# A mask table with three rows a partition: written to DRAM row by row sixteen times, read back by one DMA

## The chip, the core and the metric

The kernel runs on one core of a Trainium2 chip. The metric is the device time of one execution in microseconds: 312.74 us, the median of 3 runs (312.53 to 312.8) of the kernel before the change.

## The reference

The program computes a block-sparse attention and, on its output, a residual MLP layer. Inputs: q, k, v of 4 batches x 8 heads x 768 tokens x 64, three sampled key blocks for each of 24 blocks of 32 queries, and the MLP's weights.

```python
scores = scale * np.matmul(q, k.transpose(0, 1, 3, 2))
mask = np.abs(blk_i - blk_j) <= window          # neighbours, first and last block, sampled blocks
scores = np.where(mask, scores, -1000000000.0)
attn = np.exp(scores - max); attn = attn / (attn.sum + 1e-09); attn @ v

a1 = alpha1 * x + beta1                         # x: 4 x 768 x 512, the heads side by side
tok = np.einsum('ts,bsd->btd', w_tok, a1)
u = x + lam * tok
a2 = alpha2 * u + beta2
ch = np.maximum(a2 @ w_ch1, 0.0) @ w_ch2        # 512 -> 2048 -> 512
return u + lam * ch
```

The mask depends on the query block and the key block alone, and is the same for all batches and heads.

## The kernel before

**Tiling.** Token 6p+o lies in partition p, slot o. The 32 heads are worked on in 16 pairs. A pair's scores, keys on the partitions, are cut into nine units of 1,024 columns, two PSUM banks each. For each unit TensorE makes scores (L729 or L850), ScalarE takes the exponential into an f16 tile eT (L744 or L802), and TensorE multiplies eT with the values (L769 or L883), whose extra column of ones gives the sum; VectorE divides (L701, L704).

**Two ways to mask.** For pairs 0 to 5 the mask is in the matmul: 24 extra rows of the query operand hold 0 or -400 for each key block, and 24 extra rows of the key operand choose the block (operand rows 64 to 87, which `MB` names). For pairs 6 to 15 the two heads of a pair run side by side in a unit, and after the exponential VectorE takes the minimum of eT and a mask table, maskT, whose entries are 0 or 65504 (L807).

**The mask table.** maskT has 128 x 9 x 512 entries, that is six rows of 768 a partition, one for each slot o. It is made in three steps. `mrow` (L551) turns the 24 mask rows of a query operand into 0 and 65504 in partitions 64 to 87 of the same tile. `mout` (L557) stores these 24 rows in DRAM. `min_` (L569) reads them back with 18 DMAs on SP's queue: each fills eight partitions, 16 apart, with one row up to six times over. The tokens of partitions c, c+16, c+32, ... have the same places in their blocks of 32, so that one strided DMA does for eight partitions; two of the sixteen groups cross a block's border and take two DMAs.

**Operands by transposes.** Pairs 0 to 5 get their operands through TensorE transposes (L294) and copies (L363, L361). From pair 6 on, VectorE casts the loaded q and k into a staging tile rel (L584), and SP issues two transposing DMAs, q and k, into the operand tiles (L670). The same kind of DMA (L1010) transposes the input of the MLP from batch 1 on.

**MLP.** Token mixing is L962 (its residual add L972, its weights transposed at L506 from a load at L442), the first channel matmul L1044 with relu at L1057 (ScalarE) or L1061 (VectorE), the second L1106, the last sum L1123 and the store L1130. w2b is scaled on VectorE (L536) after its load (L472).

**Order.** A planner inside the kernel's source simulates five engines with assumed durations, and writes each engine's instructions in the order of its simulation. It also gives out the eight PSUM banks (six in one tile, one in another, one for the values' sums) and, where its model says that TensorE would stand, adds zero matmuls (`fill`, L252). `bank_order` and `pin_order` then fix the waits between engines and the order on each. SP's queue holds, in this order: the first loads, two copies of mask rows into operand tiles, mout, the 18 reads of min_, the two transposes of pair 6, those of pair 7, and then transposes and stores mixed. Loads of q, k, v and weights are issued by GpSimd (L399, L442, L464, L472), and from pair 8 on each waits for a flag that VectorE sets (L417, L397).

Of the kernel before, what the change touches and what calls it, by code (L numbers as in the profile page):

```python
# [18 lines left out]
B = 4  # L19
# [13 lines left out]
NPAIR = H // 2  # L33
VW = D + 2
UN = 1024
NU = 9
NS = NPAIR * NU
NPE = 6
NET = 11
LEADS = (18, 18, 18, 18, 18, 18, 18, 18, 19, 18, 18, 18, 18, 18, 18, 18)  # L40
PATS = (800.0, 800.0, 800.0, 800.0, 1200.0, 800.0, 0.0, 800.0, 800.0, 400.0, 800.0, 800.0, 800.0, 800.0, 800.0, 800.0)
NUDGE = {}
LOADS = (
    "v 0", "q 1", "k 1", "v 1", "q 2", "k 2", "tok 0", "tok 1", "tok 2", "v 2", "lam", "a1",
    "b1", "q 3", "v 3", "k 3", "a2", "be2", "q 4", "k 4", "v 4", "w1 0", "w1 1", "w1 2",
    "w1 3", "q 5", "k 5", "v 5", "q 6", "k 6", "v 6",
)
PR = 1
EARLY = ('b0', 'b1')
OLD = True  # L50
MROW = (2, 3, 9)
W2AT = (0, 1, 2, 7.5)
NSPLIT = 0
UTN = 0
TOKP = 1
COVER = 800.0
NLD = 6
HOLD = 2
T0 = 6600.0
MASK_AT = 28  # L60
AHEAD = 13000.0
SCALE = 1.0 / 8.0
EXPB = -0.35667494
F16MAX = 65504.0

# [71 lines left out]
def kernel(  # L137
# [69 lines left out]
    maskT = pp.tile([P, NU, 512], F16, name="maskT", tag="maskT")  # L207
# [8 lines left out]
    ps6 = ps.tile([P, 6 * 512], FP, name="ps6", tag="ps6", bufs=1)  # L216
    ps7 = ps.tile([P, 512], FP, name="ps7", tag="ps7", bufs=1)
    ps6_name = [ps6[:].tensor.name]
    BANKS = tuple(f"b{i}" for i in range(6))
    ALL = BANKS + ("b6",)  # L220
    PAIRS = ("b0+b1", "b2+b3", "b4+b5")

    def bank(name, shape, dt=FP):
        t = ps7[:, :] if name == "b6" else ps6[:, ts(ALL.index(name), 512)]
        if dt != FP:
            t = t.bitcast(dt)
        t = t[:, 0 : int(np.prod(shape[1:]))]
        return t if len(shape) == 2 else t.rearrange("p (o c) -> p o c", o=shape[1])

    def two_banks(names):  # L230
        return ps6[:, ts(PAIRS.index(names), UN)]

# [17 lines left out]
    def keep_warm(n, w, name="b6"):  # L250
        for _ in range(n):
            nc.tensor.matmul(bank(name, [P, w]), warm[:, 0:P], warm[:, 0:w], start=True, stop=True)  # L252

    def fill(ns):
        free = [x for x in ("b6", "b0", "b1") if slots[x] > 0]
        while ns > 60.0 and free:
            w = min(512, int(ns * 2.4))
            keep_warm(1, w, free[0])
            ns -= w / 2.4 + 3.0

    keep_warm(7, 512)
    keep_warm(2, P)
# [17 lines left out]
    rel0 = wk.tile([P, 2, NT, 2 * D], BF, name="rel", tag="rel", bufs=3)  # L280

    def first_cast(a):
        for i, src in enumerate((q2f, k2f)):
            sl = src[:, a, :].rearrange("p (o d) -> p o d", o=NT)
            dst = rel0[:, a, :, i * D : (i + 1) * D]
            if a == 0 and i == 1:
                nc.scalar.copy(out=dst, in_=sl)
            else:
                nc.vector.tensor_copy(out=dst, in_=sl)

    def transposes(rel, a, name, slots=range(NT)):
        tps = bank(name, [P, NT, P], BF)
        for o in slots:
            nc.tensor.transpose(tps[:, o, :], rel[:, a, o, :], identb[:])  # L294
        return tps.rearrange("p o c -> p (o c)")
# [3 lines left out]
    flatA = transposes(rel0, 0, "b0", range(0, 3))  # L299
    flatB = transposes(rel0, 0, "b1", range(3, 6))  # L300
    bqs = []
    for w in range(2):
        t = ps.tile([P, 512], FP, name="ops", tag="ops", bufs=1) if w else bank("b2", [P, 512])
# [15 lines left out]
    keep_warm(7, P)  # L319
    for j in range(2, NQB):  # L320
# [4 lines left out]

    ACT_COPY = dict(ACT=790.0)
    dma_free = [8000.0]
    SEM = 70.0  # L330
    DRAIN = 166.0
    free_at = dict(NEVER=1e9, NONE=0.0, PE=T0, ACT=T0, DVE=T0, POOL=4800.0, SP=T0)
    slots = dict(
        **{b: 1 for b in ALL}, ops=1, eT=NET, head=NQB, vext=NV, ld=NLD, rel=3,
        x=NXB, uT=3, hts=2, a1p=2, ub=2, ot=2, w2b=1,
    )
    jobs = []
    now = [0.0]

    class Job:  # L340
        def __init__(self, eng, dur, prio, fn, deps=(), take=(), give=(), lat=None):
            self.eng = eng if isinstance(eng, tuple) else (eng,)
            self.dur, self.prio, self.fn = dur, prio, fn
            self.deps = list(deps)
            self.take, self.give = take, give
            self.lat = lat
            self.alt = {}
            self.xfer = None
            self.late = 0.0
            self.moves = False  # L350
            self.done = None
            self.gate = None
            self.marks = []
            self.n = len(jobs)
            if prio in NUDGE:
                self.prio = (prio[0] + NUDGE[prio],) + prio[1:]
            jobs.append(self)

    def copy(eng, out, in_):
        if eng == "ACT":  # L360
# [4 lines left out]
    def Copy(prio, fn, deps, take=(), give=(), only=False):  # L365
        j = Job(("DVE", "NEVER") if only else ("ACT", "DVE"), 550.0, prio, fn, deps, take, give)
        j.alt = ACT_COPY
        return j

    def pieces(u):  # L370
        f = u * 512
        while f < (u + 1) * 512:
            jt, c = divmod(f, S)
            w = min(S - c, (u + 1) * 512 - f)
            yield f - u * 512, jt, c, w
            f += w

    def mmt(n, cols):
        return n * (max(cols, 60) / 2.4 + 2.7)

    def dve(n, rate, base):
        return base + n / 0.96 / rate

    pairs = [(b, n) for b in range(B) for n in range(NPAIR)]
    tl = {}
# [3 lines left out]
    def Load(xfer, prio, fn, deps=(), take=()):  # L389
        j = Job("POOL", 720.0, prio, fn, deps, take)  # L390
        j.xfer = xfer
        return j

    def load(name, src_ap, shape, dt, tag, bufs, xfer, prio, deps=(), take=(), held=None):
        def fn():
            if held is not None:
                nc.gpsimd.tensor_copy(out=held_[0:1, held : held + 1], in_=flag[0:1, held : held + 1])  # L397
            t = wk.tile(shape, dt, name=name, tag=tag, bufs=bufs)
            nc.gpsimd.dma_start(t[:], src_ap)  # L399
            return t  # L400

        return Load(xfer, prio, fn, deps, take)

    ld = {}
    wload = {}
    w2tile = []
    wtk_tile = []

    after = []
    flag = pp.tile([P, 3 * len(pairs)], BF, name="flag", tag="flag")  # L410
    held_ = pp.tile([P, 3 * len(pairs)], BF, name="held", tag="held")

    def raise_flag(p, i):
        c = 3 * p + i

        def fn():
            nc.vector.memset(flag[0:1, c : c + 1], 0.0)  # L417

        j = Job("DVE", 70.0, (0, p), fn)
        after.append((j, (p - 2) * NU + HOLD + 3 * i))  # L420
        return [j]

    def load_pair(p, prio, which="qkv"):
        for i, (src, dt, nm) in enumerate(((q, BF, "q2"), (k, BF, "k2"), (v, F16, "v2"))):
            if p == 0 and nm != "v2" or nm[0] not in which:
                continue
            hold_ = p > NPE + 1
            ld[p, nm] = load(
                nm, pair_ap(src, *pairs[p]), [P, 2, NT * D], dt, "ld", NLD,
                1300.0 if p < 2 else 980.0, prio, raise_flag(p, i) if hold_ else [], take=("ld",),  # L430
                held=3 * p + i if hold_ else None,
            )
            ld[p, nm].late = 1500.0 if hold_ else 0.0

    def plain(eng, dur, prio, fn, deps=(), **kw):
        return Job(eng, dur, prio, fn, deps, **kw)

    def load_wtk(g, prio):
        def fn():
            if g == 0:  # L440
                wtk_tile.append(wk.tile([P, NT, S], BF, name="wtk", tag="w2b", bufs=1))
            nc.gpsimd.dma_start(  # L442
                wtk_tile[0][:, 2 * g : 2 * g + 2, :],
                moe_w_tok.rearrange("(p o) s -> p o s", o=NT)[:, 2 * g : 2 * g + 2, :],
            )

        wload["tok", g] = Load(2100.0, prio, fn, take=("w2b",) if g == 0 else ())

    def load_bc(t, src, prio):
        def fn():  # L450
            nc.gpsimd.dma_start(t[:], src.unsqueeze(0).to_broadcast([P, DM]))

        return Load(720.0, prio, fn)

    def load_be2(prio):
        def fn():
            with nc.allow_non_contiguous_dma(reason="512 elements"):
                nc.gpsimd.dma_start(be2T[:], moe_beta2.rearrange("(o p) -> p o", p=P))

        return Load(200.0, prio, fn)  # L460

# [33 lines left out]
    for p in range(7, len(pairs)):  # L495
        load_pair(p, len(LOADS) + p)

# [898 lines left out]
```

## Time and profile before

| what | value |
|---|---|
| median of 3 runs | 312.74 us |
| profiled execution, first to last instruction | 307.7 us |
| its own time, launch and end included | not given apart; the median is 5.0 us above the span |
| TensorE matmul busy | 298.9 us, 97% |
| VectorE busy | 207.5 us, 67% |
| ScalarE busy | 205.8 us, 67% |
| TensorE clock granted | 1.00 |
| DMAs on SP's and ScalarE's queues | 30,940 packets, 14.61 MB |
| DMAs of GpSimd's queue | 15,984 packets, 15.47 MB |

Times in the profile count from the first instruction of the program. PE is TensorE, PEld its weight loads, DVE VectorE, ACT ScalarE, POOL GpSimd, SP SyncE; a q behind an engine's name is its queue, which issues DMAs and waits. In a line of the order of time the numbers are start and duration in us, x the count, and in brackets the idle time before it with what ended it. In a line of waits the numbers are us in total, times, and the longest.

### The profile page before, as it was taken

How to read it: one execution, taken by the hardware profiler on the slowest of the kernel's cores; microseconds unless marked ns; L12 is line 12 of the kernel's file. 1: busy time of each engine (PE TensorE's matmuls, PEld its weight loads, DVE VectorE, ACT ScalarE, POOL GpSimd, SP SyncE). 2: the span in 40 equal slices, each digit the busy share in tenths (PEclk: the TensorE clock that was granted, in tenths of full speed). 3: DMA queues.
4: the chain of work that ended last, by engine and by line, in shares of the span. 5: the costliest groups of instructions: out<-in, count | busy, mean ns of one | idle time of the engine just before them, and what ended most of it. 6: DMA issues, size and time to landing. Idle time of an engine off the chain costs nothing.

```text
span 307.7 us, 7558 instructions
## 1 busy us (share of the span) xinstructions
PE 298.9 (97%) x3161; PEld 188.1 (61%) x3194; DVE 207.5 (67%) x435; ACT 205.8 (67%) x270; POOL 52.6 (17%) x91
## 2 busy tenths in 40 slices
PE   7999999998999999999999999999999999999995
PEld 3677788674655765565656665565756656555444
DVE  4688998987889986757988696888868730010111
ACT  5999987987787567756765857766858728428000
POOL 4747323001132121211221111120000000000000
PEclk9999999999999999999999999999999999999999
DMA  5999999996453768295275834465020120010121
GB/s 147 186 253 221 213 204 210 172 125 109 69 89 66 132 71 144 51 110 110 49 134 87 128 62 111 87 87 77 3 63 34 28 29 33 34 70 0 54 84 68
DMA packets 47174, 30.81 MB, mean 100 GB/s; under 512 B 27516, under 2 KB 43044, under 8 KB 47140
## 3 DMA queue, kind: packets, MB, share of 16 engines
q0 software_dynamic: 15984, 15.47, 32.5%
q1 hardware_dynamic: 30940, 14.61, 22.7%
q8 instruction: 25, 0.41, 0.5%
q10 hardware_dynamic: 216, 0.24, 0.2%
q14 instruction: 9, 0.07, 0.1%
HBM read 32.04 MB, written 6.33 MB: 125 GB/s over the span
## 4 chain that ended last, share of the span: by engine, by line
PE 89%; DMA 6%; POOL 2%; issue 1%; ACT 1%; DVE 0%
PE ps L1044 26%; PE ps L1106 21%; PE ps L962 10%; PE ops L883 8%; PE ps L850 7%; PE ps L729 5%; PE ops L1106 5%; PE ops L769 3%; DMA wtk<-in_moe_w_tok_dram 3%; DMA kx<-rel 3%; DMA q2f<-in_q_dram 1%; PE ps L506 1%; PE ps L294 1%; PE ps L252 1%; POOL v L399 0%
## 5 line engine op out<-in xcount | busy, mean ns | idle before, releaser
L802 ACT ACTIVATE eT<-ps 128x1024 f16<-128x1024 f32 x90 | 86.9, 1023 | 32.6 <-PE ps L850 28.6
L1044 PE MATMUL ps<-uT,w1b 128*128 128x384 bf16 (+1 forms) x512 | 93.1, 326 | 0.1
L1057 ACT ACTIVATE hts<-ps,b1t 128x384 bf16<-128x384 f32 x104 | 59.9, 581 | 37.9 <-PE ps L1044 32.2
L1106 PE MATMUL ps<-w2b,hts 128*128 128x512 bf16 (+1 forms) x293 | 72.4, 373 | 1.5 <-issue 0.2
L807 DVE TENSOR_TENSOR eT<-eT,maskT 128x1024 f16<-128x1024 f16 x90 | 60.4, 687 | 17.6 <-ACT eT L802 17.5
L1044 PEld LDWEIGHTS <-w1b 128*128 128x128 bf16 x512 | 46.3, 98 | 29.0 <-ACT eT L802 1.2
L1106 PEld LDWEIGHTS <-hts 128*128 128x128 bf16 x400 | 36.6, 98 | 36.1 <-issue 2.2
L744 ACT ACTIVATE eT<-ps 128x1024 f16<-128x1024 f32 (+1 forms) x55 | 52.2, 1019 | 4.8 <-PE ps L729 4.5
L883 PEld LDWEIGHTS <-eT 128*128 128x128 f16 x720 | 30.8, 97 | 15.1 <-issue 4.0
L962 PE MATMUL ps<-a1p,wtokT 128*128 128x128 bf16 x576 | 36.6, 219 | 0.0
L883 PE MATMUL ops<-vext,eT 128*128 128x65 f16 x720 | 36.0, 193 | 0.0
L962 PEld LDWEIGHTS <-wtokT 128*128 128x128 bf16 x576 | 33.3, 98 | 2.9 <-issue 0.5
L1123 DVE TENSOR_TENSOR ot<-x_sb,ps 128x512 f32<-128x512 f32 (+1 forms) x20 | 13.4, 672 | 28.3 <-PE ps L1106 28.3
L729 PE MATMUL ps<-qx,kx 88*128 88x512 bf16 (+1 forms) x144 | 31.4, 326 | 0.6 <-ACT kx L318 0.6
L397 POOL COPY held<-flag 1x1 bf16<-1x1 bf16 x24 | 9.4, 393 | 122.5 <-DVE flag L417 122.5
L850 PE MATMUL ps<-qx,kx 64*128 64x512 bf16 (+1 forms) x240 | 25.6, 326 | 1.2 <-DMA kx<-rel 1.2
L769 PEld LDWEIGHTS <-eT 128*128 128x128 f16 x432 | 18.3, 97 | 5.0 <-DVE x_sb L704 0.6
L769 PE MATMUL ops<-vext,eT 128*128 128x65 f16 x432 | 20.2, 193 | 0.1
L972 DVE TENSOR_TENSOR x_sb<-x_sb,ps 128x384 f32<-128x384 f32 x32 | 17.5, 550 | 3.9 <-PE ps L962 3.5
L704 DVE TENSOR_TENSOR x_sb<-ops,rcp 128x384 f32<-128x384 f32 x32 | 17.8, 558 | 1.1
L1123 DVE TENSOR_TENSOR ot<-x_sb,ops 128x512 f32<-128x512 f32 (+1 forms) x5 | 3.2, 634 | 22.5 <-PE ops L1106 22.5
L850 PEld LDWEIGHTS <-kx 64*128 64x128 bf16 x240 | 8.9, 94 | 14.7 <-issue 4.4
(68 smaller groups left out, 229.5 us busy)
## 6 DMA issues: line engine op xcount, KB each, us to landing
out_dram<-ot SPq DMA_DIRECT2D x23, 256.0 KB
v<-in_v_dram POOLq DMA_DIRECT2D x16, 192.0 KB, 5.3
q<-in_q_dram POOLq DMA_DIRECT2D x15, 192.0 KB, 3.8
k<-in_k_dram POOLq DMA_DIRECT2D x15, 192.0 KB, 4.8
w1b<-in_moe_w_ch_dram POOLq DMA_DIRECT2D x4, 512.0 KB, 9.9
w2b<-in_moe_w_ch_dram POOLq DMA_DIRECT2D x4, 512.0 KB, 14.7
wtk<-in_moe_w_tok_dram POOLq DMA_DIRECT2D x3, 384.0 KB, 9.6
maskT<-mask_rows SPq DMA_DIRECT2D x14, 72.0 KB
```

Of the source, the lines that this page charges most:

```text
L704: nc.vector.tensor_tensor(out=x_sb[:, s0 : s0 + NT, h * D : (h + 1) * D], in0=op[:, :, 0:D], in1=rcp[:].unsqueeze(2).broadcast_to([P, NT, D]),
L729: nc.tensor.matmul(sps[:, f - u * UN : f - u * UN + w], kx[h][0:KC, ts(jt, P)], qx[h][0:KC, c : c + w], start=True, stop=True,)
L744: nc.scalar.activation(eT[:, c], sps[:, c], AF.Exp, bias=EXPB, scale=SCALE)
L769: nc.tensor.matmul(ops[p, a][:, t * VW : t * VW + D + 1], eTs[p, u][:, ts(i - u * GU, P)], vx[:, a, jt, 0 : D + 1], start=(i % HT == 0), s ...
L802: nc.scalar.activation(eT[:], sps[:], AF.Exp, bias=EXPB, scale=SCALE)
L807: nc.vector.tensor_tensor(out=e, in0=e, in1=maskT[:, u, :].unsqueeze(1).broadcast_to([P, 2, 512]), op=ALU.min,)
L850: nc.tensor.matmul(sps[:, a * 512 + lo : a * 512 + lo + w], kx[sl][r, ts(jt, P)], qx[sl][r, c : c + w], start=True, stop=True,)
L883: nc.tensor.matmul(ops[p, a][:, t * VW : t * VW + D + 1], eTs[p, u][:, a * 512 + c * P : a * 512 + (c + 1) * P], vx[:, a, jt, 0 : D + 1], ...
L962: nc.tensor.matmul(tp[:, j, :], wtokT[:, s, ts(3 * g + j, P)], tl["a1p", p][:, s, :], start=(s == 0), stop=(s == NT - 1),)
L1044: nc.tensor.matmul(hp[:, 0:nc_], w1b[:, dk, ts(f, P)], uTs[b][:, dk, hf * HS : hf * HS + nc_], start=(dk == 0), stop=(dk == 3),)
L1057: nc.scalar.activation(hts[kk][:, f, :], hp[:, 0:HS], AF.Relu, bias=b1t[:, f : f + 1], scale=1.0)
L1106: nc.tensor.matmul(cps[kk, mi][:, 0:w], hts[kk][:, nk, ts(m, P)], w2tile[0][:, nk, lo : lo + w], start=(nk == 0), stop=(nk == 15),)
```

## The change

The mask table becomes 128 x 3 x 1024. Tokens 6p+2g and 6p+2g+1 lie in the same block, since 32 is even, so slots 2g and 2g+1 of a partition have the same mask row: three rows a partition are enough. A unit's 512 columns can begin at column 0, 512 or 256 of a row of 768 and run over its end, so each row is 1,024 long, and its last 256 columns repeat the first.

It is made in three steps again. `M` writes the 24 rows in two VectorE instructions, 768 and 256 columns. `N` is one DMA that stores each row sixteen times, one copy for each pair of tokens, as 384 rows of 1,024 in DRAM. `O` is one DMA that reads 128 x 3,072: rows 3p, 3p+1 and 3p+2 into partition p, which lie together in DRAM.

The planner is gone. What it wrote is now a table in the source, ORDER, of words such as `e54` (the exponential of unit 54), `q54:0` (its scores, in the first two banks) or `M0`, in the order in which instructions are written. Zero matmuls are words too (`z512:6`); eleven of their places have other widths or another number of them. All eight PSUM banks are in one tile, and bank_order handles them all.

```diff
-    maskT = pp.tile([P, NU, 512], F16, name="maskT", tag="maskT")
+    maskT = pp.tile([P, 3, UN], F16, name="maskT", tag="maskT")
...
-    ps6 = ps.tile([P, 6 * 512], FP, name="ps6", tag="ps6", bufs=1)
-    ps7 = ps.tile([P, 512], FP, name="ps7", tag="ps7", bufs=1)
+    psum = ps.tile([P, 8 * 512], FP, name="psum", tag="psum", bufs=1)
...
-    rows = maskT[:].rearrange("p u c -> p (u c)")[:, 0:S]
-    mask_dr = nc.dram_tensor("mask_rows", [NBLK, S], F16, kind="Internal").ap()
-    def mrow():
-        nc.vector.tensor_scalar(
-            out=rows[MB, :], in0=qx[3][MB, :], scalar1=-1.0, scalar2=F16MAX,
-            op0=ALU.is_ge, op1=ALU.mult,
-        )
-    def mout():
-        nc.sync.dma_start(mask_dr, rows[MB, :])
-    def min_():
-        dst = maskT[:].rearrange("p u c -> p (u c)").rearrange("p (o w) -> p o w", o=NT)
-        src = mask_dr.rearrange("(m f) w -> m f w", f=3)
-        for c in range(16):
-            o = 0
-            while o < NT:
-                f, r = divmod(NT * c + o, BLK)
-                e = min(NT, o + BLK - r)
-                nc.sync.dma_start(
-                    dst[c:P:16, o:e, :], src[:, f, :].unsqueeze(1).broadcast_to([8, e - o, S])
-                )
-                o = e
+    mask_dr = nc.dram_tensor("mask_rows", [S // 2, UN], F16, kind="Internal").ap()
+    rows = maskT[:, 0, :]
+    @on("M")
+    def _(_i):
+        for c, w in ((0, S), (S, UN - S)):
+            nc.vector.tensor_scalar(
+                out=rows[MB, c : c + w], in0=qx[3][MB, 0:w], scalar1=-1.0, scalar2=F16MAX,
+                op0=ALU.is_ge, op1=ALU.mult,
+            )
+    @on("N")
+    def _(_i):
+        nc.sync.dma_start(
+            mask_dr.rearrange("(m i) w -> m i w", m=NBLK),
+            rows[MB, :].unsqueeze(1).broadcast_to([NBLK, BLK // 2, UN]),
+        )
+    @on("O")
+    def _(_i):
+        nc.sync.dma_start(maskT[:], mask_dr.rearrange("(p g) w -> p g w", p=P))
...
-            def mn(p=p, u=u):
-                e = eTs[p, u][:].rearrange("p (a c) -> p a c", a=2)
-                nc.vector.tensor_tensor(
-                    out=e, in0=e, in1=maskT[:, u, :].unsqueeze(1).broadcast_to([P, 2, 512]), op=ALU.min,
-                )
+    @on("m")
+    def _(n):
+        e = eTs[n][:].rearrange("p (a c) -> p a c", a=2)
+        g, c = divmod(n % NU * 512, 2 * S)
+        mask = maskT[:, g, c % S : c % S + 512].unsqueeze(1).broadcast_to([P, 2, 512])
+        nc.vector.tensor_tensor(out=e, in0=e, in1=mask, op=ALU.min)
...
+    def zero(w, i):
+        nc.tensor.matmul(bank(i, [P, w]), warm[:, 0:P], warm[:, 0:w], start=True, stop=True)
+    @on("z")
+    def _(w, bank_):
+        zero(w, bank_)
+    for word in ORDER.split():
+        kind = word[: next(j for j, c in enumerate(word) if c.isdigit())]
+        n, _, arg = word[len(kind) :].partition(":")
+        args = (int(arg) if arg.isdigit() else arg,) if arg else ()
+        step[kind](int(n), *args)
```

## The prediction

> **What bounds the kernel now.** I read the page first, then TensorE's waits, then a table of stretches, then the order of time around the one hole that these show.
>
> ```profile
> span 307.7 us, 7558 instructions
> PE 298.9 (97%) x3161; PEld 188.1 (61%) x3194; DVE 207.5 (67%) x435; ACT 205.8 (67%) x270; POOL 52.6 (17%) x91
> ```
>
> TensorE is busy for 298.9 of 307.7 us, so at most 8.8 us can be won without taking work from it. Its waits (us in total, times, longest) say where they lie:
>
> ```profile
> PE ps L850 <- DMA kx<-rel: 1.2, 1, 1.2
> PE ps L252 <- DVE warm L248: 1.2, 1, 1.2
> PE ps L729 <- ACT kx L318: 0.6, 1, 0.6
> ```
>
> Two are in the first 7 us. The third is the first score group of pair 6 (L850), which waits for a transposing DMA. The table of stretches (us, then busy time of each engine) puts it in place:
>
> ```profile
> 31.60:70.10 38.50, 38.38 (x564) 30.27 (x566) 35.33 (x80) 34.27 (x41) 7.43 (x10) 1.00 1.16 182
> 70.10:71.30 1.20, 0.00 (x1) 0.01 (x2) 0.79 (x2) 0.06 (x1) 0.00 (x0) 1.00 1.29 274
> 71.30:304.20 232.90, 231.25 (x2238) 138.20 (x2266) 148.46 (x300) 144.04 (x198) 25.96 (x48) 1.00 0.40 73
> ```
>
> From 31.6 to 70.1 and from 71.3 to 304.2 TensorE is full at clock 1.00; in between it does nothing for 1.2 us. What holds it is on SP, whose queue and engines around it read, in order of time:
>
> ```profile
> 40.46 0.35 DVE L551 TENSOR_SCALAR maskT<-qx 24x768 f16<-24x768 bf16 x1
> 40.84 0.31 SPq L557 DMA_DIRECT2D mask_rows<-maskT  x1
> 45.17 16.39 SPq L569 DMA_DIRECT2D maskT<-mask_rows  x18
> 55.59 0.35 DVE L584 COPY rel<-k 128x768 bf16<-128x768 bf16 x1
> 62.01 1.32 SPq L670 DMA_TRANSPOSE qx<-rel  x1
> 63.46 2.54 SPq L670 DMA_TRANSPOSE kx<-rel  x1
> 69.07 1.02 PE L1106 MATMUL ps<-w2b,hts 128*128 128x512 bf16 x3
> 71.30 0.61 PE L850 MATMUL ps<-qx,kx 64*128 64x512 bf16 x6 [1.20 <-DMA kx<-rel]
> 73.25 0.69 DVE L807 TENSOR_TENSOR eT<-eT,maskT 128x1024 f16<-128x1024 f16 x1
> ```
>
> Pair 6's staging tile is complete at 55.94 (55.59 + 0.35), but SP is still issuing the 18 mask reads until 61.56, one each 0.91 us. So both transposes start 6 us after their data is there, and the table that they queue behind is first used at 73.25.
>
> **The change, part by part.** The built programs have the same order on all five engines except for the mask steps and eleven of the zero matmuls; the PSUM banks are the same too.
>
> *SP.* Eighteen issues (16.39 us) become one. The store that fills the DRAM table stays one issue (0.31; the transposes, with twice its packets, show 1.23, and I allow that). Queued behind on SP is only pair 6's transpose, due at 55.94. It starts there unless the new read, which waits for the new store, holds SP longer. Store: 384 packets of 2 KB instead of 24 of 1.5 KB. The trace's packet records give 0.087 us for a 2 KB packet of an output store (16 DMA engines, 128 packets, 1.2 us together), and show completion writes from 12 engines for the old store, from 8 for each mask read. Twelve engines with 32 packets: 2.8 us alone. Beside the weight loads of this stretch the mask packets took 0.15 instead of 0.078, so 5.6 us at double. The old store was issued at 40.84 and its first packet came at 44.4; 0.2 us later for the new DVE part, that gives an end at 47.4 to 50.2 and an issue of the read at 48 to 51. Read: 128 packets of 6 KB, eight per engine; the nearest rows are 0.25 us (token weights, 3 KB written from 6 KB) and 0.32 (w1, 4 KB from 8 KB), so 2.0 to 2.6 alone, 5.2 at double; with the 3.9 us that the first mask read took to its first packet, it ends at 54 to 60. The table is needed at 72: 12 us spare. SP is free by 51, 5 us before the transpose is due.
>
> The Trainium skill, "SBUF — State Buffer", section Door 1, speaks against this store: DMA rate depends on how many of 16 ports the partitions reach, and by its table partitions 64 to 87 reach six. At its 27.2 GB/s a port, an estimate from the page is 4.8 us for 786 KB, which lies inside 2.8 to 5.6 and changes nothing in the sum.
>
> *The two transposes.* They are issued at about 56.0 and 57.3 instead of 62.01 and 63.46. Alone, two such transposes (1536 packets of 256 B) took 1.9 us (104.2 to 106.1 in the packet records). Beside loads they crawl: from 78.5 to 80.5 one transpose went out with about one packet for each load packet. At 57 loads are still queued (w2 and pair 7, landing from 59.6 to 70.1). The mask reads of before sat on 8 engines, 99 packets of 0.078 each, 7.7 us; the new table costs 12 engines 2.8 + 2.0 = 4.8 and the other four 2.0, so the slowest engines get rid of their loads sooner. Bounds for the landing: 60 if the loads did not matter; 70.7 if the transposes came through only once the last load is off, as in before (loads off at 69.5; pair 6's last 650 packets then took until 70.4 and the first matmul came at 71.30, 0.9 later; with most packets already through, some 0.3 + 0.9 after 69.5). I take 67, nearer the upper end, because one packet for each load packet passes 96 per engine before the loads end.
>
> The Trainium skill, "DMA: Bandwidth & Descriptors", section Queues, rings and completion order, states that each DMA engine takes turns between queue rows packet by packet. That agrees with the interleaving above; taken strictly it would make the early transposes slow pair 7's load by one short packet each.
>
> *What TensorE gains.* The last L1106 matmul before the hole starts at 69.72 and takes 0.215; the next matmul after a change to L850 usually comes 0.095 later than its length asks. So pair 6 can begin at 70.03, against 71.30: **1.27 us**. Its PSUM banks are free (exponentials of the units before end at 69.2, the residual add on bank 1 at 68.34). What is late next: ScalarE's exponential of the unit before ends at 70.16, before the new scores are there; DVE is idle from 70.89 to 72.54; both wait for TensorE here and move with it. From 71.3 on nothing but TensorE's own work (231.25 of 232.90) sets the pace, so the shift lasts to the end, where the tail of 3.5 us after the last matmul is unchanged.
>
> *DVE.* One more tensor_scalar, 24x256: between 0.16 (the smallest DVE copies here) and 0.35 (24x768); 0.2. Behind it stands a residual add that waited 0.15 for TensorE, then the shift of pair 2's operand, used at 44.19 with 1.8 us to spare: 0. The min with the mask keeps its form, 90 x 0.687: 0.
>
> *Zero matmuls.* They shrink by 1,826 columns net; at 0.215 per 512 that is 0.77 us of TensorE. All but two lie before 31.4, where ScalarE runs without a hole (eight exponentials in 7.61 us from 25.08), and TensorE then waits 0.25 for it at 31.14: they become waiting. The two at 53.9 to 55.3 stand before transposes which start at 55.66, when ScalarE's copy of the last ones (54.78 + 0.80) frees the bank: 0. If those covers failed, the gain would be up to 0.13 for the latter, 0.64 for the former.
>
> *Waits.* The first score matmul now waits for ScalarE's step that ends at 6.10 instead of 6.59, up to 0.5 earlier; but TensorE stands at 17.6 for the token weights (landed 17.58), which don't move: 0. ScalarE's relus lose waits for DVE's; TensorE, which is full there, gains nothing.
>
> Sum: 307.7 - 1.27 = 306.4 of span. The runs' median is 312.74, 5.0 above the profiled span, and no time of that execution alone is given; I take the 5.0 as fixed: **311.5 us**.
>
> **The rivals.** A: *the transposes land late anyway.* If they come through only with the last load, at 70.7 at the latest, the gain is 0.6 or less: 312.1 to 312.7. For it: 63.3 to 69.5 shows them nearly stopped. Against: most of that stood behind mask packets until 66.6. B: *the store is the new wait* (slower). It reads each of 24 rows 16 times over; if these packets took turns instead of spreading over 12 engines, 384 x 0.087 = 33 us would put its end at 78, the read and the transposes behind it on SP, and the hole at some 15 us: 328. It decides from an end of the store at about 61, where SP is as late as now. Against: a packet of one partition took 0.078 as store or load. C: *pair 7's load.* It landed at 61.97 for a DVE cast at 62.56; the burst of mask and transposes comes ahead of it now. DVE has 0.72 idle behind that cast and TensorE about 0.5 more before it needs pair 3's operand (66.59). From a landing at 63.8 each us costs one. On the slowest engines the new table's 4.8 us and 96 transpose packets of 0.031 (3.0) now come before it, against some 72 mask packets of 0.078 (5.6) then: 2.2 us later at most, 64.2; I take half, 63.1. At 66 the gain is gone and 0.9 lost: 313.7. D: *more*, if the earlier start or the zeros count: 310.9.
>
> **How the numbers follow.** Full gain 0.67, A 0.16 (a quarter of it still beyond 0.2%), B 0.05, C 0.09 (half of it near no change), D 0.03. A measurement here can tell about 0.2%, 0.63 us. Faster: 0.67 + 0.04 + 0.03 = 0.74; within: 0.12 + 0.04 = 0.16; slower 0.10. The range goes from D, 310.9, over A into C, 312.9; the likeliest case alone spans 311.1 to 311.9.
>
> **What would show it.** Right: the page's PE wait on kx gone, SP's transposes for pair 6 at 56 to 57, TensorE's stretch from 31 to 303 without a hole, the span at 306.4. Wrong: an SP wait at the mask read past 56 (B), a DVE wait for q near 62.6 and TensorE idle near 66 (C), or a shorter wait on kx at 70 (A).

## The result, and the profile after

The kernel after takes 308.04 us (median of 4 executions, 307.76 to 309.19), the kernel before beside it 312.63 (311.66 to 312.8): a ratio of 0.9886 with a 95% interval of 0.9849 to 0.9924. Three later measurements of the unchanged pair gave 0.9887 [0.9856, 0.9919], 0.9889 [0.9859, 0.9919] and 0.9912 [0.9879, 0.9946]. The forecast was 311.5 with a range of 310.9 to 312.9. Its direction was right; its gain, 1.27 us, was less than a third of what came.

The first page of the kernel after:

```profile
span 306.0 us, 7521 instructions
PE 299.4 (98%) x3161; PEld 188.1 (61%) x3192; DVE 207.7 (68%) x436; ACT 205.7 (67%) x270; POOL 52.3 (17%) x91
```

TensorE's waits (us in total, times, longest) no longer hold one on kx:

```profile
PE psum L298 <- DVE warm L295: 1.2, 1, 1.2
PE psum L460 <- DMA wtk<-in_moe_w_tok_dram: 0.3, 1, 0.3
PE psum L792 <- issue: 0.2, 1, 0.2
```

The table of stretches (us, busy time of PE, PEld, DVE, ACT and POOL, then granted clock, DMA share, GB/s), cut where it was cut before:

```profile
31.60:70.00 38.40, 38.35 (x566) 30.21 (x566) 35.39 (x81) 33.95 (x41) 7.41 (x11) 1.00 1.22 208
70.00:71.30 1.30, 1.30 (x25) 0.83 (x25) 0.92 (x3) 1.00 (x2) 0.00 (x0) 1.00 0.00 0
71.30:302.60 231.30, 229.66 (x2215) 137.50 (x2242) 148.53 (x300) 143.33 (x198) 25.95 (x48) 1.00 0.41 72
```

The row in the middle is the old hole: TensorE was busy for none of it and is busy for all of it now. The order of time shows why, SP first, then TensorE:

```profile
52.63 0.35 SPq L506 DMA_DIRECT2D maskT<-mask_rows  x1
53.82 1.36 SPq L554 DMA_TRANSPOSE qx<-rel  x1
56.01 3.10 SPq L554 DMA_TRANSPOSE kx<-rel  x1
...
69.06 1.02 PE L792 MATMUL psum<-w2b,hts 128*128 128x512 bf16 x3
70.02 0.61 PE L595 MATMUL psum<-qx,kx 64*128 64x512 bf16 x6
```

Pair 6's transposes are issued 7 to 8 us earlier than at 62.01 and 63.46, and its scores begin at 70.02 instead of 71.30. So this profiled execution did what the forecast said (a span of 306.4), and its span is 1.7 us shorter than the one before (306.0 against 307.7). Yet the medians differ by 4.6 us. The experiments ask where the rest is.

In what follows every execution comes with its span, and its time is 1.72 to 1.84 us above it, in all 125 executions of the kernel before that were measured beside the experiments and all 20 of the kernel after. The 5.0 us that the forecast took for time outside the span are not there. The profiled execution of before (307.7, so some 309.5 us) lies at the low end of a kernel whose executions spread from 309.2 to 313.6 (clock is an execution's mean granted TensorE clock). Two executions of before, 314.5 and 315.1 us at a clock of 0.988, count as slow and are left out here and below:

```
kernel before, 123 executions: 309.2 to 310.9 us   27, clock 0.998 or more
                               310.9 to 311.2       2, clock 0.998 or more
                               311.2 to 312.9      49, clock 0.998 or more
                               310.0 to 313.6      45, clock 0.995 or less (median 312.5)
kernel after, 20 executions:   307.4 to 308.3      10, clock 0.998 or more
                               308.7 to 309.2      10, clock 0.998 or more
```

Over all of these the medians are 311.64 and 308.54, 3.1 us apart; that the first measurement gave 4.6 was in part a draw of long executions of before.

### The profile page after: what moved, and what is told of

Same layout as the page of the kernel before. It is cut to its first block, busy times and chain, and to the rows that moved or that the text cites. A ratio compares the mean times of both kernels' runs of the same rounds, so it can differ in the third digit from the quotient of the medians.

```text
span 306.0 us, 7521 instructions
## 1 busy us (share of the span) xinstructions
PE 299.4 (98%) x3161; PEld 188.1 (61%) x3192; DVE 207.7 (68%) x436; ACT 205.7 (67%) x270; POOL 52.3 (17%) x91
## 4 chain that ended last, share of the span: by engine, by line
PE 92%; DMA 4%; POOL 2%; issue 1%; ACT 1%; DVE 0%
PE psum L758 27%; PE psum L792 27%; PE psum L619 12%; PE psum L704 11%; PE psum L595 7%; PE psum L585 6%; DMA wtk<-in_moe_w_tok_dram 3%; DMA q2f<-in_q_dram 1%; PE psum L335 1%; PE psum L460 1%; POOL v L402 0%; PE psum L298 0%; POOL q L402 0%; POOL k L402 0%; PE psum L740 0%
## 5 line engine op out<-in xcount | busy, mean ns | idle before, releaser
L605 ACT ACTIVATE eT<-psum 128x1024 f16<-128x1024 f32 (+1 forms) x145 | 139.0, 1021 | 36.5 <-PE psum L595 27.6
L758 PE MATMUL psum<-uT,w1b 128*128 128x384 bf16 (+1 forms) x512 | 93.1, 326 | 0.1
L792 PE MATMUL psum<-w2b,hts 128*128 128x512 bf16 (+1 forms) x371 | 86.7, 370 | 1.6 <-issue 0.2
L772 ACT ACTIVATE hts<-psum,b1t 128x384 bf16<-128x384 f32 x104 | 60.4, 583 | 37.4 <-PE psum L758 33.4
L619 PE MATMUL psum<-vext,eT 128*128 128x65 f16 x1152 | 56.2, 193 | 0.0
L704 PE MATMUL psum<-a1p,wtokT 128*128 128x128 bf16 x576 | 36.6, 219 | 0.0
L585 PE MATMUL psum<-qx,kx 88*128 88x512 bf16 (+1 forms) x144 | 31.4, 326 | 0.1
L595 PE MATMUL psum<-qx,kx 64*128 64x512 bf16 (+1 forms) x240 | 25.6, 326 | 0.0
L653 DVE TENSOR_TENSOR x_sb<-psum,rcp 128x384 f32<-128x384 f32 x32 | 17.8, 558 | 1.1
L720 DVE TENSOR_TENSOR ub<-x_sb,a_bc 128x384 bf16<-128x384 f32 x32 | 17.7, 552 | 0.1
L595 PEld LDWEIGHTS <-kx 64*128 64x128 bf16 x240 | 8.9, 94 | 13.4 <-issue 4.5
```

The lines of the kernel that those rows point to most:

```text
L585: nc.tensor.matmul(t[:, f : f + w], kx[h][0:KC, ts(jt, P)], qx[h][0:KC, c : c + w], start=True, stop=True,)
L595: nc.tensor.matmul(t[:, a * 512 + f : a * 512 + f + w], kx[h][r, ts(jt, P)], qx[h][r, c : c + w], start=True, stop=True,)
L605: nc.scalar.activation(eTs[n][:, c], t[:, c], AF.Exp, bias=EXPB, scale=SCALE)
L619: nc.tensor.matmul(ops[p, a][:, t * VW : t * VW + D + 1], eTs[n][:, c : c + P], vext[p % NV][:, a, jt, 0 : D + 1], start=(jt == t == 0), s ...
L653: nc.vector.tensor_tensor(out=x_sb[:, s0 : s0 + NT, h * D : (h + 1) * D], in0=t[:, :, 0:D], in1=rcp[:].unsqueeze(2).broadcast_to([P, NT, D ...
L704: nc.tensor.matmul(t[:, j, :], wtokT[:, s, ts(3 * g + j, P)], a1p[p][:, s, :], start=(s == 0), stop=(s == NT - 1),)
```

## The experiments

In this part the table is ORDER, the planner's is the program that writes its order itself, and the hole is the stretch in which TensorE stands ahead of pair 6.

**Which part of the change does it?** Four kernels on one chip: before, after, and the two mixed ones. The old mask in the kernel with the ORDER table:

```diff
-    maskT = pp.tile([P, 3, UN], F16, name="maskT", tag="maskT")
+    maskT = pp.tile([P, NU, 512], F16, name="maskT", tag="maskT")
...
-        nc.sync.dma_start(maskT[:], mask_dr.rearrange("(p g) w -> p g w", p=P))
+        for c in range(16):
...
+                nc.sync.dma_start(
+                    dst[c:P:16, o:e, :], src[:, f, :].unsqueeze(1).broadcast_to([8, e - o, S])
+                )
```

> The table source with the old mask steps: one store of 24 rows and 18 reads; zero matmuls, banks and waits as changed. Theory 'mask alone': 312 to 312.8, as before, with TensorE's wait for pair 6's transposes back. Theory 'table': the gain beyond 1.3 us comes from the other zero matmuls and waits, so about 309.3. Theory 'outside': the time lies some 5 us above the span again if the number of DMAs issued decides that.

The new mask steps in the kernel with the planner (the same lines the other way):

> The planner's source with nothing but the mask steps changed (its order, zero matmuls and waits as before). Theory 'mask alone': 308 us, as the changed kernel. Theory 'table': 311.3 (1.3 us below before).

Before and after, unchanged:

> The kernel before, unchanged. The change took 4.6 us off the median where 1.3 us of the profiled span were forecast, and the changed kernel's executions all lie 1.8 us above their span. Theory 'body': the kernel before also spends 1.8 us outside its span, its usual executions have spans of 310 to 311 us, and the profiled one (307.7) was a lucky one; a new profile shows a longer wait than 1.2 us of TensorE for pair 6's transposes, up to 4.5. Theory 'outside': each execution's time lies 5.0 us above its span, spans stay at 307.7.

> The changed kernel, unchanged, on the same chip as the others: 308 us, span 306.2, time 1.8 us above its span, no wait for pair 6's transposes; one execution in four may be 1 us longer, as the first four were.

Measured, against the kernel before: unchanged 0.999 [0.9958, 1.0022]; old mask in the table 311.47 us, 0.9995 [0.9959, 1.0032]; new mask in the planner 308.17, 0.9928 [0.9888, 0.9968]; after 308.4, 0.9887 [0.9856, 0.9919]. The old mask keeps its wait in the table's program too:

```profile
PE psum L601 <- DMA kx<-rel: 1.2, 1, 1.2
```

The new profile of before, an execution of 309.74 us, has a wait on kx of 0.9 us, not the longer one that 'body' expected. In all four kernels time and span differ by 1.72 to 1.85 us, so what is won is won inside the span. In the medians the table alone brings nothing that can be told, the new mask most. But the new mask in the planner's program has two groups, six executions at 307.7 to 308.2 and four at 310.9 to 311.4; the kernel after has only the first and some near 309. That the source is worth nothing can't be said yet.

**What sets the executions of before apart?** Two more profiles of the unchanged kernel:

> The kernel before, unchanged, for another profiled execution. Executions of it took from 309.5 to 313.4 us, and about one in three reports a mean TensorE clock of 0.992 to 0.995 where the kernel after reports 0.999 to 1.000. Three theories for an execution above 311.3 us. CLOCK: the hole at pair 6 makes the clock fall to half for 3.4 us, so the profile shows a clock below 1.00 in a stretch after 70 us and about 1.7 us lost there. HOLE: the wait on kx is itself longer than in the first profile, 2.5 us or more instead of 1.2. START: the loss lies in the first 14 us, where TensorE reaches full rate later, and exponential 16 starts 2 us later than at 21.7. If this execution is a short one (309.5 to 310.5), all three say the same: a wait of 0.9 to 1.3 and no loss elsewhere.

> The same kernel and the same three readings as for b2_before_look: CLOCK a stretch after 70 us below full clock, HOLE a wait on kx of 2.5 us or more, START a late exponential 16.

The first caught one at a mean clock of 0.993 (311.76 us). Its wait on kx:

```profile
PE ps L850 <- DMA kx<-rel: 2.0, 1, 2.0
```

and its stretches (cut at the hole and where the clock changes):

```profile
66.00:69.90 3.90, 3.90 (x55) 2.72 (x53) 3.77 (x10) 3.29 (x4) 0.00 (x0) 1.00 1.33 115
69.90:73.35 3.45, 1.44 (x25) 0.91 (x25) 1.00 (x3) 1.08 (x3) 0.00 (x0) 1.00 1.07 108
73.35:76.77 3.42, 3.42 (x20) 1.54 (x18) 1.85 (x5) 2.58 (x4) 1.23 (x2) 0.50 0.21 26
```

The second row holds the hole; in the third TensorE is busy throughout, at a granted clock of 0.50. CLOCK holds for this execution, and HOLE in part: the hole is 0.8 us longer than in the first profile, and the fall behind it costs 1.57 us more (against the first profile its exponential 56 starts 0.69 later, exponential 60 then 2.26 later, and so to the end). Exponentials are counted here from 0, in the order in which ScalarE ran them, and serve as marks of how late an execution is. Below, an execution whose clock drops to half behind a hole has fallen.

The second profile, 311.5 us at a clock of 1.000, has no wait on kx:

```profile
PE ps L252 <- DVE warm L248: 1.2, 1, 1.2
PE ps L729 <- ACT kx L318: 0.2, 1, 0.2
```

Here exponential 16 starts at 24.95 instead of 21.67 (START). TensorE runs at half rate for longer; the same two matmuls in the first profile, and in this one:

```profile
8.79 0.60 PE L252 MATMUL ps<-warm 128*128 128x512 bf16 x2
```

```profile
11.29 1.06 PE L252 MATMUL ps<-warm 128*128 128x512 bf16 x2
```

This is called a late start below. TensorE comes to pair 6 3.28 us late, when the transposes have landed, and so gets 1.27 us back. So the long executions of before are, by these two profiles, of two kinds, and such a late start hides the hole.

**SP's issues, or the reads' load on the DMA engines?** The old 18 reads, with pair 6's transposes after the eleventh:

```diff
-r43 q46:2 S1 tq6 tk6 r44 e45
+r43 q46:2 S1 tq6 tk6 O1 r44 e45
...
+        for c, o, e, f in (reads[:11], reads[11:])[i]:
+            nc.sync.dma_start(
```

> The old table of 24 rows and its 18 reads, same bytes and packets as before, but pair 6's two transposes stand after the 11th read on SP instead of after the 18th. Theory ISSUE (SP's 16.4 us of issues held the transposes back): they are issued at 56 to 58, the wait on kx is gone or under 0.3 us, and the median is that of the kernel after, 308.0 to 308.6 us, with a clock of 0.999 to 1.000 in every execution. Rival LOAD (it is the old reads' packets on the DMA engines that keep the transposes from coming through, wherever they are issued): kx still lands after 69.5, the wait is 0.6 us or more, and the median is 310.5 to 311.6 as in the kernel before.

SP in order of time:

```profile
46.80 9.23 SPq L514 DMA_DIRECT2D maskT<-mask_rows  x11
56.55 1.54 SPq L562 DMA_TRANSPOSE qx<-rel  x1
58.20 3.23 SPq L562 DMA_TRANSPOSE kx<-rel  x1
61.48 7.24 SPq L514 DMA_DIRECT2D maskT<-mask_rows  x7
```

No wait on kx is left: their 1536 packets are out by 68.3, against the 69.1 that an early start would need (its scores can begin at 70.03, and the first matmul of before came 0.9 us behind the last packet). ISSUE holds in this, with all the old bytes still there, and no execution of 12 falls below a clock of 0.998. The time is 309.6 us, 0.994 [0.9909, 0.997], a microsecond more than expected; 0.44 of it is the end of the program, which is looked at last. The profiled execution had a late start (exponential 16 at 23.03). What else holds the others up was not looked at.

**What does a hole cost?** The kernel after, with the cast of pair 6's keys and their transpose put later:

```diff
-e42 r41 z384:6 H11:1 ck6 f0:0 cv6 ...
+e42 r41 z384:6 H11:1 f0:0 cv6 ...
-r43 q46:2 S1 tq6 tk6 r44 e45 ...
+r43 q46:2 S1 tq6 r44 e45 ...
-q53:1 x8 ... e53 S3 q54:0 q55:2 ...
+q53:1 x8 ... e53 S3 ck6 tk6 q54:0 q55:2 ...
```

> The kernel after with the cast of pair 6's keys, and their transpose, moved behind a later multiply on VectorE, so that the transpose is issued near 70 us and lands near 72.5: a hole of about 2.5 to 3.2 us comes back at pair 6, twice that of the kernel before, without its 18 reads. Theory CLOCK: the clock falls to half behind the hole in most executions, reported as 0.992 to 0.995, and the time is 308.2 + 2.9 + 1.7 = 312.8 us. Rival (the hole costs its own length and no more): 308.2 + 2.9 = 311.1 us at a clock of 0.999 to 1.000. If half of the executions fall, the times come in two groups 1.7 us or more apart.

```profile
71.00:73.82 2.82, 0.32 (x4) 0.20 (x6) 0.89 (x2) 0.00 (x0) 0.00 (x0) 1.00 0.37 70
73.82:77.24 3.42, 3.42 (x28) 1.46 (x26) 1.91 (x5) 1.94 (x2) 1.08 (x2) 0.50 0.00 0
```

These stretches of its profile are the same picture without any of the 18 reads: a wait of 2.7 us, then half clock for 3.41. Ten of 12 executions report 0.993 to 0.995; the median is 312.56 us, as CLOCK said. The same with a shorter delay ("cv7 ck6 tk6 r51" in the table):

> As in the run with the late key cast, but the cast and its transpose stand one step earlier, behind the cast of pair 7's values: issued near 69 us, landing near 71, a hole of 1.2 to 1.9 us. Theory CLOCK: what decides is how much of one period of 3.41 us the hole fills; a hole of 1.2 did not make the clock fall in two profiles, one of 2.0 and one of 2.7 did; so here a quarter to a half of the executions show 0.992 to 0.995, against ten of twelve with the longer hole, and the early, unfallen ones lie at 309.3 to 310.0. Rival: the fall comes from something else in the 24-row kernels, the 18 reads; then no execution here falls.

Its wait is 1.6 us, and none of 7 executions fell: 309.81 us. That is what the rival says too, but the ten falls of the longer delay came without the 18 reads and rule it out. The mechanism stands, the share that I expected here does not. The trace records when the clock rises, and the rises and falls in one execution lie whole periods of 3.413 us apart, so each hole can be laid against its period. A fall came where a wait filled 59% (2.0 of 3.41 us) and 78% (2.7) of one period; none came at 25 to 37% (0.9 to 1.27), at 47% (1.6), nor for a hole of 2.4 us that a period's end cut, its larger part filling 52%.

**The start.** First more executions of the kernel after, and the holes of TensorE's first 6 us filled:

```diff
-    for _ in range(2):
+    for _ in range(4):
         zero(P, 6)
...
+    for _ in range(2):
+        zero(P, 6)
     bqs = []
...
-    for _ in range(7):
+    for _ in range(8):
         zero(P, 6)
```

> The kernel after, unchanged, for more executions. Theory START: TensorE's early matmuls run at half rate (0.43 us for 512 columns instead of 0.215) until 4.1 to 5.6 us in some executions and until 9.5 to 13.7 us in others, by where the clock's periods of 3.41 us fall; in the profiles so far the late ones cost 1.2 to 1.7 or 3.2 us by exponential 16. Then the times of this kernel come in groups at 307.5 to 308.2, 309.0 to 309.7 and 310.9 to 311.4 us, all at a clock of 0.998 or more, and the first eight executions (five, three, none) were a lucky draw: the median may be as high as 309.5. Rival: this kernel starts early by what the change does, and nine in ten executions lie below 309.3.

> The kernel after with five more zero matmuls of 128 columns around TensorE's first transposes: two ahead of them, two behind, one more ahead of the first scores, to fill the 0.2 to 0.3 us holes that TensorE has from 4.57 to 6.3 us. Theory START: a period of 3.41 us must be nearly full for the clock to rise; with these holes filled the period that ends at 6.0 to 7.4 us passes too, so the rise comes at 4.1 to 7.4 in nearly every execution, the groups at 309.0 to 309.7 and 310.9 to 311.4 us thin out to one in ten or two, and the median is 307.9 to 308.5. The extra matmuls themselves cost at most 0.3 us. Rival (late starts have another cause, a load for one): the groups stay as they are, all 0 to 0.3 us later.

> The same five zero matmuls in the kernel with the ORDER table and the old mask steps (24 rows, 18 reads). If they make the start early in nearly all executions, this one meets its hole at pair 6 in nearly all of them too: 309.6 to 310.3 us where the clock does not fall and 311.2 to 312.2 (at 0.992 to 0.995) where it does, against 307.9 to 308.5 for the new mask. So at equal starts the change is worth 1.7 to 2 us without and 3.3 to 4 with a fall. Rival (the change is worth the 1.3 us of the first profile, the rest being the draw of starts): the medians of the two differ by 1.2 to 1.5 us.

After: 308.75 us, no execution above 309.0, so the third group did not show, and START in this form (late starts cost every kernel the same) is refuted. The profiled execution started early. Instead it lost 1.2 us (against the first profile of before) from exponential 16 to 24, in a wait for x_sb: a late start is not the only thing that makes the group at 309. VectorE, which makes x_sb, stood before it for a load:

```profile
24.94 0.69 DVE L470 TENSOR_TENSOR a_bc<-a_bc,lam_bc 128x512 f32<-128x512 f32 x1 [1.43 <-DMA a_bc<-in_moe_alpha_dram]
...
27.25 0.56 DVE L653 TENSOR_TENSOR x_sb<-psum,rcp 128x384 f32<-128x384 f32 x1
```

TensorE's wait for x_sb, 0.2 to 1.3 us, is in the profiles of nine of the table's ten early starts (variants included), in none of its late starts and in none of the planner's three early ones; whether the table is the cause wasn't tested. The filled start: 308.34 us (308.04 to 309.54), with a profile where the clock rises at 7.16 and exponential 16 is 0.1 late; six executions are too few to call that better than the kernel after. The filled start with the old mask: 311.03 us, with a wait of 2.4 us on kx in its profile and 4 of 12 executions fallen. With these matmuls in both, the new mask is worth 2.7 us of median, though it isn't shown that the starts are then equal; of the two readings the first is nearer.

The profiles of late starts differ by program: half rate until 9.5 to 10.4 us in the table's, until 13.4 and 13.7 in the planner's. The planner's first score matmul waits for ScalarE's copy of the keys, the table's does not. To put that wait back, two of ScalarE's steps were changed about:

```diff
+    nc.scalar.copy(out=kx[0][0:D, HS:S], in_=flatB[D:P, HS:S])
     nc.scalar.activation(
...
-    nc.scalar.copy(out=kx[0][0:D, HS:S], in_=flatB[D:P, HS:S])
```

> The kernel after with two of ScalarE's first steps changed about, so that its last step ahead of the first score matmul ends 0.5 us later, as in the kernel before; all else is unchanged. Theory RISE: with the hole that this makes on TensorE from 6.6 to 7.1 us, the period of 3.41 us that ends near 10 fails as well when the one that ends near 6.5 has failed, and the clock rises at 13.4 to 13.7 instead of 9.5 to 10.4 us. Then a third to a half of the executions lie at 310.5 to 311.4 us, where the kernel after has none of 14, and the rest stay at 307.4 to 309.2. Rival (the step is worth its 0.5 us at most, which the wait for the token weights at 17.6 swallows): all executions stay below 309.7.

> The same kernel again, for more executions and a second profile. RISE: a third to a half at 310.5 to 311.4 us. Rival: none. In a profile of a late execution the first 512-column matmul at 0.215 us comes after 13 us by RISE, at 9.5 to 10.4 by the rival.

> The kernel after beside them on the same chip. RISE: late starts come as often, but cost 1.2 to 1.7 us, so all executions lie between 307.4 and 309.3. If some lie at 310.5 or more here too, the first 14 were a lucky draw and RISE isn't shown by the others.

All 16 executions stayed below 309.4 (medians 308.33 and 308.2; after beside them 308.6). By what was expected RISE is refuted, but the edit may have missed its mark: no profile caught it in a late start, and by the other kernels' late starts ScalarE has a wait of 0.27 us ahead of this step there, which the swapped copy would fill. So the hole need not have existed in the executions that matter; this is argued, not shown. The next edit holds TensorE itself:

```diff
-    for _ in range(7):
+    for _ in range(6):
         zero(P, 6)
+    nc.tensor.matmul(bank(6, [P, P]), kx[0][0:D, HS : HS + P], warm[0:D, 0:P], start=True, stop=True)
```

> The kernel after, with the last of the seven zero matmuls ahead of the first scores taking its weights from the second half of the first keys (times zeros, so nothing that is used changes). TensorE then stands until ScalarE's copy ends: near 6.9 us where the clock is up, near 7.5 where it is not, a hole of 0.3 to 0.5 us. Theory RISE: where the clock missed its rise near 6 to 7 us (6 of 17 profiles) the period that ends near 10 is now too empty as well, the rise comes at 13 to 14 us, and these executions lie at 310.5 to 311.6 us; the rest stay at 307.5 to 309.5. So about a third of the executions lie above 310.4, where the kernel after has none of 20. Rival (the wait costs its 0.5 us at most): all executions stay below 309.9.

> The same kernel for more executions and another profile. RISE: about a third above 310.4 us, and a profile of one of these shows half-rate matmuls until 13 to 14 us. Rival: none above 309.9.

Eight of 21 executions lie at 310.7 to 311.2 us, where the kernel after has none of 20 (medians of the two runs 309.51 and 309.22). (Three more report a clock of 0.994, at 309.2 to 309.6 us; where theirs fell was not seen.) TensorE's order of time in a late start of the kernel after (the third of the runs beside the swapped steps):

```profile
8.78 0.85 PE L335 MATMUL psum<-identb,rel 128*128 128x128 bf16 x6
9.41 0.65 PE L298 MATMUL psum<-warm 128*128 128x512 bf16 x2
...
10.34 0.60 PE L298 MATMUL psum<-warm 128*128 128x512 bf16 x2
```

and in the second run held on the keys:

```profile
7.41 0.28 PE L362 MATMUL psum<-warm,kx 64*128 64x128 bf16 x1 [0.32 <-ACT kx L359]
...
9.95 1.06 PE L298 MATMUL psum<-warm 128*128 128x512 bf16 x2
...
11.66 1.06 PE L298 MATMUL psum<-warm 128*128 128x512 bf16 x2
...
13.69 0.60 PE L586 MATMUL psum<-qx,kx 88*128 88x512 bf16 x2
```

Two matmuls of 512 columns take 1.06 us at half rate and 0.60 at full. The kernel after is at full rate by 9.5 us; with a wait of 0.32 us at 7.1 it is not before 13.0, and its exponential 16 starts 3.11 us late instead of 1.15 (against the first profile of the kernel after, 21.71). The new mask in the planner's program shows the same, with the wait that the table removed:

```profile
PE ps L252 <- DVE warm L248: 1.2, 1, 1.2
PE ps L725 <- ACT kx L318: 0.2, 1, 0.2
```

Its exponential 16 is 3.13 late. RISE holds: where the first rise is missed, a wait of 0.2 to 0.3 us on the keys makes the next period miss it too.

**The tail.** From the last matmul's start to the end, all profiles with the 18 reads take 3.80 to 3.82 us, all with one read 3.37 to 3.39. One DMA more on SP, without the reads:

```diff
-        nc.sync.dma_start(maskT[:], mask_dr.rearrange("(p g) w -> p g w", p=P))
+        back = mask_dr.rearrange("(p g) w -> p g w", p=P)
+        nc.sync.dma_start(maskT[0:64], back[0:64])
+        nc.sync.dma_start(maskT[64:P], back[64:P])
```

> The kernel after with the one long read of the mask table split in two DMAs of 64 partitions each, so SP issues one DMA more. Theory COUNT: the last output store now counts the semaphore that SP looks at second at the end instead of ninth, the seven looks behind it (0.06 us each) come after the store has landed instead of before, and from the last matmul's start to the end it takes 3.81 us instead of 3.38, with no hole at pair 6; the times lie 0.4 us above those of the kernel after, median 308.4 to 309.0. Rival (the 0.44 us belong to the 18 reads themselves, their semaphores or their packets): the tail stays at 3.38.

VectorE's last step in the kernel before, after, and with the read in two (each fence begins with the span):

```profile
core 0 of [0], span 307.7 us
...
304.22 0.42 DVE L1123 TENSOR_TENSOR ot<-x_sb,ps 128x256 f32<-128x256 f32 x1 [1.33 <-PE ps L1106]
```

```profile
core 0 of [0], span 306.0 us
...
302.93 0.42 DVE L802 TENSOR_TENSOR ot<-x_sb,psum 128x256 f32<-128x256 f32 x1 [1.32 <-PE psum L792]
```

```profile
core 0 of [0], span 307.9 us
...
304.36 0.42 DVE L804 TENSOR_TENSOR ot<-x_sb,psum 128x256 f32<-128x256 f32 x1 [1.32 <-PE psum L794]
```

From there to the end: 3.5, 3.1 and 3.5 us. COUNT holds: the last matmul to the end takes 3.81 again. SP's wait at the end for the last store, in the same order, in us:

```profile
SPq L1391 <- DMA out_dram<-ot: 1.3, 1, 1.3
```

```profile
SPq L852 <- DMA out_dram<-ot: 0.9, 1, 0.9
```

```profile
SPq L854 <- DMA out_dram<-ot: 1.3, 1, 1.3
```

In the trace of the kernel after SP's ninth look is the one that stands until the store has landed (305.09, landed 305.07); with the read in two it is the second (306.53, landed 306.51), and seven looks follow. The median, 309.51 us (0.9942 [0.9905, 0.9978]), is above what was expected: in its profile a wait of 0.9 us on kx came back (a weight load landed at 71.2 there), and one execution fell to 0.993; the others were not looked at.

## Why the prediction was wrong

**The base of the sum: the step that failed.** "I take the 5.0 as fixed." Only 1.8 us of it lies outside the span. The other 3.2 set the profiled execution apart from the median by events inside other executions. On the profiled execution's own time the sum was nearly right: 309.5 - 1.27 is 308.2, and the kernel after's profiled execution took 307.76. The median moved further because the change removes or shortens much of what made the other executions longer. That the two profiled executions were so alike is luck: both were early starts that had not fallen, a group with 27 of the 123 executions of before.

**The fall of the clock, not in the sum.** 45 of 123 executions of before report a clock of 0.995 or less, and none of after. Where it was profiled it cost 1.57 us; over all executions that is 0.6 (45/123 x 1.57). The hole was costed at its own length, from a profile in which it was 1.27 us long and filled too little of a period.

**"Waits: 0".** This step weighed the earlier first score matmul against the token weights at 17.6, and in an early start that is right: exponential 16 starts at 21.67 and 21.71. In a late start the wait costs about 1.9 us (3.1 to 3.3 against 1.1 to 1.4 late). Late starts are about two fifths of the executions, by the groups of the kernel held on the keys (8 of 21), of the planner's with the new mask (4 of 10) and of before at 311.2 us and more without a fall (49 of 123). With the old mask the shorter late start wins less: the profile of the old mask in the table has one (exponential 16 at 22.83, not 24.95), and there TensorE reaches pair 6 before kx and waits 1.2 us.

**"The tail of 3.5 us after the last matmul is unchanged."** It shrank by 0.44 us, in every profile.

**What was right.** TensorE's gain, 1.27 us: from exponential 56 on the profiled execution runs 1.27 to 1.36 ahead of the one before. The transposes' landing: forecast 67, measured 67.77 for kx. Their 1536 packets were out by 66.5, ahead of the last weight load's landing at 67.56, so they did come through between load packets. They were issued at 53.82 and 56.01, the first 2 us earlier than forecast, since it waits for q's half of the staging tile alone. Rival C did not come: pair 7's load landed at 61.64, forecast 63.1. Rival B did not come, though the store was slower than its upper bound: issued at 40.97, with the read that waits for it at 52.63, not by 51. Rival A showed in two profiles of variants (waits on kx of 0.6 and 0.9 us with the new mask). Rival D named the early start, but put it at 0.6 us.

Together: 0.44 of tail, 0.6 of fall, two fifths of 1.9 for the start (0.75), and three fifths of a hole of 0.9 to 2.4 (1.5 at the mean of five profiles, 0.9) make an estimate of 2.7 us, where the means over all executions differ by 3.1 (311.56 against 308.42). The waits for x_sb work against it: from exponential 16 to 24 the table's ten profiled early starts lose 0.4 us in the mean. The rest is open, as is how often each start comes.

## What to carry to other kernels

Set the profiled execution's own time beside the spread of all runs before working from it: here they differed by a constant 1.8 us, and the rest of the gap to the median meant that other executions held events which that profile didn't show. A short hole on TensorE has two prices, its length and, if it fills well over half of one clock period (59% did here, 52% did not), the half-rate period behind it, 1.57 us. A wait in the first microseconds is not free because a later wait swallows it; ask whether TensorE has reached full rate by then.

## What the runs showed of the hardware

- The clock's records end and begin whole periods apart: 300.373 us at full clock in the kernel after is 88 periods of 3.413. In the 20 profiles a rise took about three quarters of a period: with each matmul weighted by the rows it uses of 128, the periods that ended in a rise had a busy share of 0.75 and more, those that did not 0.77 and less. Falls came with 59 and 78% of one period idle, none with 52% or less.
- The Trainium skill, "TensorE: Matmul & The Clock Gate", Part 1, gives a free-running window of 3.41 us, and half rate after an idle window. The period agrees. The fall does not need a whole idle window: 59% of one was enough here.
- The clock column reads 1.00 before the first rise is recorded. In the new mask's run in the planner's program it shows 1.00 at 9 to 10 us, while two matmuls of 512 columns take 1.06 us just before and after (at 8.00 and 11.35). Only the matmuls' lengths tell a late start.

```profile
9.00:10.00 1.00, 1.00 (x9) 0.72 (x7) 0.27 (x1) 0.91 (x1) 1.00 (x3) 1.00 1.50 160
```

- One DMA more or less on SP's queue can move the end by 0.44 us: which semaphore the last store counts depends on how many DMAs came before it (one or 17 more gave SP's second look here instead of its ninth), and at the end SP looks at all of them one after another, 0.06 us each, in one fixed order. Looks that stand ahead of the last store's pass while it is under way; those behind it come after it has landed.
